# Attention, mixture of experts and a squared-ReLU network: eight squares put on another engine, and three groups of output weights prepared at earlier products

## The chip, the cores and the metric

The kernel runs on one core of one Trainium2 chip. The metric is the time of one execution on the device in microseconds (us). TensorE multiplies matrices, VectorE and GpSimd do element-wise work on tensors, ScalarE applies functions to them, and SyncE issues most of the transfers. Each engine takes its instructions strictly in the order of the program, and waits on semaphores for what other engines deliver.

## The reference: what is computed

Three networks follow one another: windowed attention (4 batches, 8 heads, 576 positions, width 64), a mixture of 8 experts with two chosen per token, and a dense network whose hidden values are squared after a ReLU. The change lies in the last one:

```python
def _moe2_ref(x, w_in, w_out):       # x 2304 x 512, w_in 512 x 2048, w_out 2048 x 512
    h = x @ w_in
    r = np.maximum(h, 0.0)
    g = r * r
    return (g @ w_out).astype(np.float32)
```

## The kernel before, in words

**Layers and products.** The last network works on three blocks of 768 tokens. Both of its layers use a recursive scheme with seven products in place of eight for a 2 x 2 split of the matrices. Its products are called 1 to 7 in the code, and their sums give four quarters of the result. Every operand is held as two numbers, a high part (a copy rounded on ScalarE) and a low part (the rest, mostly a subtraction on VectorE), so that each product is done in three passes: high by high, high by low, low by high. A high or low part is made by the operations that `split` (line 846) lists and `do` (line 870) issues, and so nearly all of these stand under line 872 in the profile.

**First layer.** The program walks 24 groups (3 blocks of 8, `NG`), seven products each. `product` (line 1155) does product "1" into PSUM tile `psa` and copies it to `tt` on ScalarE (line 1161), product "2" into `psc`, "6" on top of `psa` with a copy to `wt` (line 1169), "5" into `psb`, "7" on top of `psa` with a copy to `tt` (line 1176), "4" on top of `psa`, and "3" on top of `psb`. A product that adds to `psa` must wait until ScalarE has copied the sum before it. Each group gives four quarters, which are passed through ReLU and square and stored to DRAM (`gmid`). Three of them (quarters 0, 2 and 3, after products "2", "7" and "3") go through `g_sum` (line 1063): VectorE adds the PSUM tile and the copy (line 1065), and squares the positive part in place in one further VectorE instruction (line 1066). Quarter 1 (product "4") goes through two ScalarE instructions, Relu (line 1182) and Square (line 1183). A group's last two products, "4" and "3", stand among the first products of the next group; those of the last group come after all others.

**Second layer.** It takes 36 batches of 14 products (`mul_out`, line 1199), and reads as operands the stored quarters of two hidden groups (`g_load`, on SyncE's queue), their sums (`g_adds`, GpSimd), and the high and low parts of both (`g_split`: parts 0 and 2 on ScalarE, 1 and 3 on VectorE). Its buffers hold three batches. `g_split(n, 1)` also issues the load for batch n + 3.

**Slots.** What runs beside the products is set by hand. After each product `step` (line 1142) issues the side work listed under the number of that product, its slot. Product "1" of group g is slot 7g. The first layer's slots end at 167; the last products "4" and "3" follow without slots of their own; `end` = 168 is the first slot of the second layer, and batch n of it has slots 168 + 14n to 168 + 14n + 13. Side work of the same slot is issued in the order in which it was listed in the program.

**Output weights.** They are kept in eight groups, and take the places of the input weights of the same number. Each group is prepared in four pieces of 512, 512, 512 and 256 columns by eight steps (`w_sums`, line 892). An even step asks for the transfer of the piece after next (`w_load`, line 877, tile `raw`, on GpSimd's queue, four buffers) and makes the high part on ScalarE. An odd step makes the low part on VectorE. Groups 0 to 4 are done at slots 126 to 160 (line 1132), groups 5 to 7 at slots 168 + 20(k - 5) + (0, 2, 5, 7, 10, 12, 15, 17) for group k (lines 1211 and 1212). The low parts of group 5 so stand at slots 170, 175, 180 and 185, of group 6 at 190, 195, 200 and 205, of group 7 at 210, 215, 220 and 225. Batch 4 of the second layer needs group 5, batch 5 needs groups 6 and 7.

```python
    def g_sum(s, k, q, ps, u):
        t = g_tile()
        nc.vector.tensor_tensor(out=t, in0=ps, in1=u, op=OP.add)
        nc.vector.scalar_tensor_tensor(out=t, in0=t, scalar=0.0, in1=t, op0=OP.max, op1=OP.mult)
        g_to(s, k, q, t)
```

Of the kernel before, what the change touches and what calls it, by code (L numbers as in the profile page):

```python
# [16 lines left out]
AF = mybir.ActivationFunctionType  # L17
OP = mybir.AluOpType
# [31 lines left out]
def attn_moe_ffn(ctx: ExitStack, tc: tile.TileContext, qt, kt, vt, wgn, noise, w1, w2, w_in, w_out,  # L50
                 consts, out):
    nc = tc.nc
# [18 lines left out]
    def bank(tag):  # L71
        if tag == "b":
            return psum.tile([128, 2, 512], F32, name="psb", tag="b", bufs=2)
        return psum.tile([128, 512], F32, name="ps" + tag, tag=tag, bufs={"a": 3, "c": 1}[tag])
# [440 lines left out]
    for p in range(NT // 2):  # L515
        v = 4 * p + 3
        end = v == last
# [374 lines left out]
    def w_sums(k, out_w):  # L892

        steps = []
        for j in range(4):
            m, st = 4 * (8 * out_w + k) + j, {}

            def high(m=m, j=j, st=st):
                w_load(max(m + 3, 4))
                n_i = min(2, 7 - 2 * j)  # L900
                st[0] = split(WP[k], 2 * j, [w_buf(m)[:, 0:256 * n_i].rearrange("p (i n) -> p i n", n=256)], "dve")
                do(st[0][0])

            steps += [high, lambda st=st: do(st[0][1])]
        return steps
# [146 lines left out]
    NSB = N // SB  # L1052

    def g_to(s, k, q, t):
        nc.sync.dma_start(out=gmid[s, k, :, :, q, :].rearrange("u p n -> p u n"),
                          in_=t.rearrange("p (u n) -> p u n", u=3))

    def g_tile():
        ng[0] += 1
        n = (ng[0] - 1) % 4  # L1060
        return tmp[4 + n // 2] if n % 2 == 0 else rows.tile([128, DM], F32, name="yo", tag="yo", bufs=2)[:, 0:HALF]

    def g_sum(s, k, q, ps, u):
        t = g_tile()
        nc.vector.tensor_tensor(out=t, in0=ps, in1=u, op=OP.add)
        nc.vector.scalar_tensor_tensor(out=t, in0=t, scalar=0.0, in1=t, op0=OP.max, op1=OP.mult)
        g_to(s, k, q, t)


# [38 lines left out]
    def on(slot, f, *a):  # L1108
        side.setdefault(slot, []).append((f, a))

    def on_all(slots, steps):
        for m, f in zip(slots, steps):
            on(m, f)
# [3 lines left out]
    for s in range(NSB - 1):  # L1117
        for i in range(6):
            t, m = 6 * (s + 1) + i, 56 * s + 5 * i + 3
# [9 lines left out]
    out_sums = [w_sums(k, 1) for k in range(8)]  # L1129
    end = 56 * NSB  # L1130
    for k in range(5):
        on_all([end - 56 + 7 * (k + 2) + m for m in (0, 1, 2, 3, 3, 4, 5, 6)], out_sums[k])
    for n in range(3):
        on(end - 48 + 8 * n, g_load, n)
        for m in range(2):
            on(end - 20 + 4 * n + 2 * m, g_adds, n, "pool", m)
# [18 lines left out]
    def product(g, p):  # L1155
# [6 lines left out]
        elif p == "2":  # L1162
            b = bank("c")[:, :HALF]
            mul_in(P2, k, b, True, True)
            g_sum(s, k, 0, b, t)
        elif p == "6":
            a = LIVE["a", g]
            mul_in(P6, k, a, False, False)
            nc.scalar.activation(out=u2, in_=a, func=AF.Copy)
        elif p == "5":  # L1170
            LIVE["c", g] = c = bank("b")[:, 0, :HALF]
            mul_in(P5, k, c, True, False)
        elif p == "7":
            a = LIVE["a", g]
            mul_in(P7, k, a, False, False)
            nc.scalar.activation(out=u3, in_=a, func=AF.Copy)  # L1176
            g_sum(s, k, 2, LIVE["c", g], u3)
        elif p == "4":
            a = LIVE.pop(("a", g))
            mul_in(P4, k, a, False, True)  # L1180
            t = g_tile()
            nc.scalar.activation(out=t, in_=a, func=AF.Relu)
            nc.scalar.activation(out=t, in_=t, func=AF.Square)
            g_to(s, k, 1, t)
        else:
            c = LIVE.pop(("c", g))
            mul_in(P3, k, c, False, True)
            g_sum(s, k, 3, c, u2)
# [16 lines left out]
    for n in range(len(batches)):  # L1205
# [2 lines left out]
                on(end + 14 * n + 1 + 4 * m, g_adds, n + 3, "pool", m)  # L1208
        for m in range(4):
            on(end + 14 * n + (2, 5, 8, 11)[m], g_split, n + 2, m)  # L1210
    for k in range(5, 8):
        on_all([end + 20 * (k - 5) + m for m in (0, 2, 5, 7, 10, 12, 15, 17)], out_sums[k])
    BANKS = {}
    two = lambda ap: ap.rearrange("p (k n) -> p k n", k=2)
    twice = lambda ap: ap[:, None, :].to_broadcast([128, 2, 256])
    for n, (s, u, kk) in enumerate(batches):
        if kk == 0:
            if (3 * s + u) % 2:
                t = [bank("b") for _ in range(2)]
# [91 lines left out]
```

## Time and profile before

| What | Value |
|---|---|
| Time, median of 3 runs (lowest, highest) | 978.65 us (977.57, 979.04) |
| Profiled execution: time on the device | 978.19 us |
| Profiled execution: span from first to last instruction | 976.1 us |
| TensorE busy in the span | 957.3 us, 98% |
| VectorE busy | 674.8 us, 69% |
| ScalarE busy | 463.8 us, 48% |
| GpSimd busy | 419.2 us, 43% |
| Granted TensorE clock, mean over the span | 0.998 |

PE is TensorE, PEld its weight loads, DVE VectorE, ACT ScalarE, POOL GpSimd, SP SyncE. A row of the timeline gives the start in us from the span's start, the length in us, the engine, the line, the operation, output tile <- input tiles with their shapes, how many instructions are merged in the row, and in brackets how long the engine was idle before it and what ended that. An engine can begin an instruction a little before the one ahead has ended, so the distance between two starts is what an instruction costs its queue.

The first layer of the last network's third block (groups 16 to 23) runs from about 726 to 787 us; the second layer runs from 787 us to the end.

### The profile page before, as it was taken

The page shows a single profiled execution, that of the slowest core. Times are in us where ns is not written, and L with a number is a line of the kernel's source. Part 1 is how long each engine was busy: PE and PEld are TensorE (multiplying, and loading weights), DVE is VectorE, ACT ScalarE, POOL GpSimd, SP SyncE. Part 2 cuts the span into 40 slices and gives each one's busy share as a digit, 9 for nine tenths or more (in the row PEclk, how much of TensorE's full clock was granted, in tenths as well). Part 3 has the DMA queues.
Part 4 walks back from the last instruction along what each step waited for, and adds up shares of the span by engine and source line. Part 5 has one row for each costly group of instructions (what it writes and reads, how often), then busy time and mean ns, then how long its engine had stood idle before and what let it go on. Part 6 is the DMA issues. An engine that isn't in the chain of part 4 may idle for free. (4 is left out here: it accounts for less than half of the span.)

```text
span 976.1 us, 19647 instructions
## 1 busy us (share of the span) xinstructions
PE 957.3 (98%) x7438; PEld 879.1 (90%) x7438; DVE 674.8 (69%) x1432; ACT 463.8 (48%) x887; POOL 419.2 (43%) x453
## 2 busy tenths in 40 slices
PE   8899999999999999999999999999999999999998
PEld 6677779898998989899898898999999998999998
DVE  5777754757686776766764436778576999877773
ACT  6677743434343343433343446655554564434331
POOL 0665543124242333425334032624221667988880
PEclk9999999999999999999999999999999999999999
DMA  8777525456667575656555453976538774444331
GB/s 277 273 237 279 198 88 152 135 166 226 197 212 241 161 234 197 219 204 207 202 190 200 148 174 94 299 203 181 151 99 240 227 213 156 145 140 129 130 108 44
DMA packets 118198, 179.99 MB, mean 184 GB/s; under 512 B 11232, under 2 KB 66288, under 8 KB 117712
## 3 DMA queue, kind: packets, MB, share of 16 engines
q1 hardware_dynamic: 107120, 146.77, 46.9%
q0 software_dynamic: 10976, 31.90, 10.6%
q8 instruction: 59, 0.97, 0.4%
q14 instruction: 43, 0.35, 0.1%
HBM read 124.33 MB, written 54.30 MB: 183 GB/s over the span
## 5 line engine op out<-in xcount | busy, mean ns | idle before, releaser
L872 POOL TENSOR_TENSOR gs<-xb 128x256 f32<-128x256 f32 x72 | 69.5, 985 | 29.3 <-DVE wc L872 13.0
L476 ACT ACTIVATE ha<-psa 128x384 fp32r<-128x384 f32 x64 | 31.3, 491 | 93.3 <-PE psa L472 91.8
L268 ACT ACTIVATE p<-p,mx 128x192 f32<-128x192 f32 x144 | 57.6, 450 | 30.3 <-DVE mx L262 29.5
L689 POOL TENSOR_TENSOR et<-ex,et 128x512 f32<-128x512 f32 x16 | 20.9, 1304 | 112.3 <-DVE ex L685 112.3
L710 POOL DMA_INDIRECT yr<-yg,pos x36 | 36.1, 1003 | 68.4 <-DVE ha L477 44.9
L477 DVE SCALAR_TENSOR_TENSOR ha<-psa,ha 128x384 fp32r<-128x384 f32 x64 | 35.4, 553 | 43.0 <-ACT ha L476 38.0
L428 POOL DMA_INDIRECT slots<-tok,pos x36 | 35.0, 972 | 46.1 <-DVE rs L314 29.6
L472 PE MATMUL psa<-xa,wa 128*128 128x384 f32 x288 | 53.4, 336 | 0.3 <-DVE ha L477 0.3
L472 PE MATMUL psa<-xa,wc 128*128 128x384 f32 x288 | 53.4, 336 | 0.0
L791 PE MATMUL psb<-wa,ha 128*128 128x512 f32 x216 | 52.8, 396 | 0.0
L441 POOL DMA_INDIRECT xr<-xd,gidx x40 | 44.3, 1108 | 19.2 <-issue 6.0
L262 DVE CUSTOM_DVE_ANT_0 p<-psb,bias 128x192 f32<-128x192 f32 x144 | 45.8, 352 | 7.7 <-PE psb L257 6.8
L472 PEld LDWEIGHTS psa<-xa,wa 128*128 128x128 f32 x288 | 49.4, 188 | 0.6 <-DVE ha L477 0.5
L472 PEld LDWEIGHTS psa<-xa,wc 128*128 128x128 f32 x288 | 49.6, 188 | 0.2
L795 ACT ACTIVATE yo<-psb 128x512 f32<-128x512 f32 x38 | 22.7, 598 | 54.3 <-PE psb L791 40.8
L872 DVE TENSOR_TENSOR wc<-gs,wc 128x512 fp32r<-128x512 f32 x48 | 48.5, 1049 | 0.0
L689 POOL TENSOR_TENSOR ex<-ex 128x512 f32<-128x512 f32 x12 | 15.6, 1303 | 74.8 <-DVE ex L685 74.8
L886 POOL DMA_DIRECT2D raw<-w x49 | 27.2, 560 | 47.0 <-DVE wb L872 18.4
L791 PEld LDWEIGHTS psb<-wa,ha 128*128 128x128 f32 x216 | 39.5, 188 | 7.8
L791 PE MATMUL psb<-wb,ha 128*128 128x512 f32 x176 | 46.3, 398 | 0.0
L110 DVE TENSOR_TENSOR wa<-raw,wa 128x1024 fp32r<-128x1024 f32 x20 | 25.3, 1266 | 30.0 <-ACT wa L106 29.9
L303 PEld LDWEIGHTS psb<-v,pt 64*64 64x64 f32 (+1 forms) x1056 | 33.1, 136 | 11.6 <-issue 7.9
(327 smaller groups left out, 2742.6 us busy)
## 6 DMA issues: line engine op xcount, KB each, us to landing
raw<-in_w_dram SPq DMA_DIRECT2D x64, 512.0 KB, 5.3
xb<-gmid SPq DMA_DIRECT2D x72, 256.0 KB, 2.7
v<-in_vt_dram SPq DMA_DIRECT2D x20, 520.0 KB, 6.7
yg<-yo SPq DMA_DIRECT2D x40, 256.0 KB, 2.5
raw<-w POOLq DMA_DIRECT2D x36, 256.0 KB, 3.9
gmid<-yo SPq DMA_DIRECT2D x48, 192.0 KB
ex<-in_w_in_dram SPq DMA_DIRECT2D x16, 512.0 KB, 4.4
ex<-in_w_out_dram SPq DMA_DIRECT2D x16, 512.0 KB, 3.4
```

Of the source, the lines that this page charges most:

```text
L262: nc.vector.tensor_tensor_reduce(out=p2[j][:, a, :], in0=ps[:, a, j, :], in1=bias[:, 4 * g + 2 * j + a, :], op0=OP.add, op1=OP.min, scale= ...
L268: nc.scalar.activation(out=p2[j][:, a, :], in_=p2[j][:, a, :], func=AF.Exp, bias=mx[j][:, a:a + 1], scale=-1.0)
L303: nc.tensor.matmul(px[64 * x:64 * x + 64, a, j, :], l, r, start=not any(m[:2] == (x, a) for m in mms[:n]), stop=not any(m[:3] == (x, a, j) ...
L428: st = nc.gpsimd.indirect_dma_start(out=slots, out_offset=bass.IndirectOffsetOnAxis(ap=pos[:, i, k:k + 1], axis=0), in_=tok[:, i:i + 1], i ...
L441: nc.gpsimd.indirect_dma_start(out=XR[e, j], out_offset=None, in_=xd[0:PARTS[j] * 128] if early else xd, in_offset=bass.IndirectOffsetOnAx ...
L472: nc.tensor.matmul(o, w[wp][:, f * 128:(f + 1) * 128], x[:, xp, d, :], start=(n == 0), stop=(n == 11))
L476: nc.scalar.activation(out=hi, in_=ps, func=AF.Relu)
L477: nc.vector.scalar_tensor_tensor(out=lo, in0=ps, scalar=0.0, in1=hi.bitcast(F32), op0=OP.max, op1=OP.subtract)
L689: nc.gpsimd.tensor_tensor(out=x, in0=af, in1=cf, op=OP.add)
L710: nc.gpsimd.indirect_dma_start(out=YR[i, k], out_offset=None, in_=yg, in_offset=bass.IndirectOffsetOnAxis(ap=pos[:, i, k:k + 1], axis=0))
L791: nc.tensor.matmul(py, h[:, hq], wc[wp][:, wsl], start=(f + n == 0), stop=(f == 7 and n == 2))
L872: f(**a)
```

## The change

Two edits. In the third block, quarter 0 is no longer squared by one VectorE instruction but by a Relu and a Square on ScalarE, in place; VectorE keeps the addition ahead of them. And the steps of output-weight groups 5, 6 and 7 are listed under slots 161 + 21(k - 5) + (0, 2, 5, ...): group 5 seven slots sooner than before, group 6 six, group 7 five. They are also listed earlier in the program, so that in a slot shared with `g_load`, `g_adds` or `g_split` they now come first.

```diff
@@ -1063,7 +1063,11 @@
     def g_sum(s, k, q, ps, u):
         t = g_tile()
         nc.vector.tensor_tensor(out=t, in0=ps, in1=u, op=OP.add)
-        nc.vector.scalar_tensor_tensor(out=t, in0=t, scalar=0.0, in1=t, op0=OP.max, op1=OP.mult)
+        if s == NSB - 1 and q == 0:
+            nc.scalar.activation(out=t, in_=t, func=AF.Relu)
+            nc.scalar.activation(out=t, in_=t, func=AF.Square)
+        else:
+            nc.vector.scalar_tensor_tensor(out=t, in0=t, scalar=0.0, in1=t, op0=OP.max, op1=OP.mult)
         g_to(s, k, q, t)
 
 
@@ -1130,6 +1134,8 @@
     end = 56 * NSB
     for k in range(5):
         on_all([end - 56 + 7 * (k + 2) + m for m in (0, 1, 2, 3, 3, 4, 5, 6)], out_sums[k])
+    for k in range(5, 8):
+        on_all([end - 7 + 21 * (k - 5) + m for m in (0, 2, 5, 7, 10, 12, 15, 17)], out_sums[k])
     for n in range(3):
         on(end - 48 + 8 * n, g_load, n)
         for m in range(2):
@@ -1208,8 +1214,6 @@
                 on(end + 14 * n + 1 + 4 * m, g_adds, n + 3, "pool", m)
         for m in range(4):
             on(end + 14 * n + (2, 5, 8, 11)[m], g_split, n + 2, m)
-    for k in range(5, 8):
-        on_all([end + 20 * (k - 5) + m for m in (0, 2, 5, 7, 10, 12, 15, 17)], out_sums[k])
     BANKS = {}
```

## Rows read from the trace of the kernel before

**Rows 1.** Busy time by stage: PE, PEld, DVE, ACT, POOL, clock, DMA share, GB/s

```profile
773.00:787.10 14.10, 13.52 (x79) 13.20 (x78) 13.68 (x21) 9.10 (x19) 5.81 (x9) 1.00 0.79 229
787.10:807.00 19.90, 19.90 (x169) 19.90 (x168) 19.83 (x20) 12.09 (x22) 16.75 (x22) 1.00 0.65 192
807.00:820.10 13.10, 11.00 (x87) 10.36 (x86) 13.10 (x14) 7.01 (x14) 10.81 (x12) 1.00 0.34 111
```

**Rows 2.** All waits of TensorE from 780 us to the end: total us, times, longest

```profile
PE psa L1201 <- DVE ex L872: 1.2, 1, 1.2
PE psa L1201 <- DVE wc L872: 0.9, 1, 0.9
PE psa L1046 <- ACT tt L1176: 0.6, 1, 0.6
```

**Rows 3.** Timeline of TensorE, 775 to 821 us

```profile
775.66 1.20 PE L1046 MATMUL psa<-wc,wa 128*128 128x384 f32 x6
...
777.74 1.20 PE L1046 MATMUL psc<-wc,ha 128*128 128x384 f32 x6
...
784.73 1.34 PE L1046 MATMUL psa<-ex,ha 128*128 128x384 f32 x6 [0.58 <-ACT tt L1176]
...
786.94 1.59 PE L1201 MATMUL psa<-wb,wc 128*128 128x256 f32 x12
...
797.01 5.20 PE L1201 MATMUL psb<-wb,ex 128*128 128x256 f32 x42
...
820.13 2.68 PE L1201 MATMUL psb<-ha,wc 128*128 128x256 f32 x21
```

**Rows 4.** Timeline of ScalarE, 774 to 788 us

```profile
774.26 0.47 ACT L1169 ACTIVATE wt<-psa 128x384 f32<-128x384 f32 x1
...
780.07 0.49 ACT L1182 ACTIVATE yo<-psa 128x384 f32<-128x384 f32 x1 [1.64 <-PE psa L1046]
780.59 0.53 ACT L1183 ACTIVATE yo<-yo 128x384 f32<-128x384 f32 x1
781.02 0.83 ACT L872 ACTIVATE wc<-xb 128x768 fp32r<-128x768 f32 x1
781.76 0.47 ACT L1169 ACTIVATE wt<-psa 128x384 f32<-128x384 f32 x1
782.13 1.14 ACT L872 ACTIVATE wc<-gs 128x512 fp32r<-128x512 f32 x2
783.17 0.83 ACT L872 ACTIVATE wc<-xb 128x768 fp32r<-128x768 f32 x1
784.18 0.49 ACT L1176 ACTIVATE tt<-psa 128x384 f32<-128x384 f32 x1 [0.18 <-PE psa L1046]
...
787.05 0.62 ACT L872 ACTIVATE wa<-raw 128x512 fp32r<-128x512 f32 x1
```

**Rows 5.** Line 1066, 728 to 788 us: ns min/median/max, first and last start

```profile
L1066 DVE SCALAR_TENSOR_TENSOR tt<-tt x8: 557/558/1621, 729.4 to 781.2; 128x384 f32<-128x384 f32 x8
```

**Rows 6.** Timeline of VectorE, 772 to 817 us

```profile
772.93 0.55 DVE L1065 TENSOR_TENSOR tt<-psc,tt 128x384 f32<-128x384 f32 x1
...
773.99 2.12 DVE L872 TENSOR_TENSOR ha<-raw,ha 128x512 fp32r<-128x512 f32 x1
...
780.61 0.55 DVE L1065 TENSOR_TENSOR tt<-psc,tt 128x384 f32<-128x384 f32 x1
...
787.14 0.56 DVE L1065 TENSOR_TENSOR yo<-psb,wt 128x384 f32<-128x384 f32 x1
...
790.89 1.23 DVE L872 TENSOR_TENSOR wa<-raw,wa 128x512 fp32r<-128x512 f32 x1
...
816.18 0.95 DVE L872 TENSOR_TENSOR wa<-raw,wa 128x256 fp32r<-128x256 f32 x1
```

**Rows 7.** GpSimd's issue of a weight piece, and such transfers' time to landing

```profile
776.41 0.54 POOL L886 DMA_DIRECT2D raw<-w  x1 [0.86 <-DVE ha L872]
...
raw<-w POOLq DMA_DIRECT2D x6, 256.0 KB, 3.4
```

## The prediction

> **What bounds the kernel now.** I read the busy time by stage first [rows 1]. From 787.10 us, where the second layer begins, VectorE is busy for 19.83 of 19.90 us and then for all of 13.10 us, while ScalarE works 54 to 61% of the time; TensorE works through the first of these stretches without a gap and lacks 2.10 us in the second. So at the start of the second layer VectorE is the bound, and that is where the moved weight pieces stand. In the stretch ahead, 773 to 787 us, VectorE is nearly as full (13.68 of 14.10 us), yet TensorE loses only 0.58 us.
>
> The list of TensorE's waits says what these gaps are [rows 2]: two in the second layer, for low parts made by VectorE (0.9 us in batch 4, 1.2 us in batch 5), and one of 0.6 us at the end of the first, for ScalarE's copy of line 1176. No other wait of TensorE stands between 780 us and the end, so whatever shift remains when batch 6 begins is carried to the end. The timeline of TensorE bounds what can be won [rows 3]: from the start of batch 0 (786.94) to that of batch 6 (820.13) are 33.19 us. The first two, which lie ahead of both waits, take 10.07 us (batch 2 begins at 797.01), so six take 30.21 us with no wait. All that VectorE costs here is thus 2.98 us, and with the wait ahead of it 3.56 us, or 0.36%. What this kernel's measurement can tell from no change is about 0.2%, 1.96 us.
>
> One more reading carries the argument. VectorE's first instruction of the second layer's stretch is the sum for the last product "3" (787.14) [rows 6]. It starts 0.20 us after TensorE began on the second layer (786.94) [rows 3], as soon as that product has drained, though VectorE was all but full up to then. VectorE has caught up at this point, and what it saves earlier it would spend here, waiting for TensorE. I call this the meeting point, and count all that follows from it.
>
> **Squares moved.** Eight VectorE instructions of 0.558 us each in the median [rows 5] go, 4.5 us over a stretch of 52 us. Ahead of the meeting point that is worth nothing to TensorE, whose only loss there is to ScalarE [rows 1, 2]. What is added are eight pairs on ScalarE. The pair of lines 1182 and 1183 has the same tile: 0.52 us from the first start to the second, 0.43 us from there to the next instruction, 0.95 us together [rows 4]. Work of that size would fit into ScalarE's idle time. But the Relu has to wait for VectorE's sum, and everything listed behind it on ScalarE waits too. Among that are the copies for which TensorE's next product on `psa` waits (lines 1169 and 1176).
>
> In the last group, 23, this can be added up. Its product "2" begins at 777.74 and ends at 778.94 [rows 3]; VectorE adds only at 780.61 and is done at 781.16 [rows 6]. Until now ScalarE went on meanwhile: line 1182 at 780.07, line 1169 at 781.76, line 1176 at 784.18, done at 784.67 [rows 4]. With the change the queue from the sum's end to the end of line 1176 is, by distances of starts [rows 4]: Relu 0.52, Square 0.43, line 1182 0.52, line 1183 0.43, high part of batch 0's own operands 0.74, line 1169 0.37, its sums 1.04, the high part of group 5's second weight piece, now at slot 166, 0.53 (787.05 to the next row's start), batch 1's own high part 0.74, line 1176 itself 0.49: 5.81 us. From 781.16 that ends at 786.97, 2.30 us later than now. The last product "4" waits for just this copy (784.73, 0.58 us idle) [rows 3], and so the meeting point moves by 2.30 us.
>
> The end of the sum is the uncertain part. From below: VectorE has no backlog and adds as soon as product "2" ends, at 779.49; then the copy ends at 785.30, +0.63 us. With one square less ahead of it, 780.60: +1.74 us. From above: group 22 is itself held up. There the sum ends at 773.48 [rows 6]; Relu, Square, lines 1182 and 1183, a weight piece (0.53) and line 1169 (0.47) end at 776.38, where line 1169 now starts at 774.26, and the product that waits for it began at 775.66 [rows 3]: TensorE loses 0.7 us there, and the sum of group 23 can slip by as much, to 781.86: +3.0 us. I take 781.16: the 0.56 us saved are given back where VectorE's low part of a weight piece waits for its high part, which ScalarE brings 0.95 us later behind each added pair. The value 2.30 is nearest to the row as it stands.
>
> **Weight pieces moved.** Three things are moved: transfers, high parts, low parts. The transfer for the piece at slot 161 leaves GpSimd at 776.41 as before and lands 3.4 us later [rows 7], at 779.8; its high part (0.53) then ends at 780.3, ahead of the sum that ScalarE must wait for anyway, and costs nothing; if that transfer were 1.3 us later, it would cost up to 0.5 us. Its low part, at slot 163, falls where VectorE waits for ScalarE's late high part of batch 0. The later transfers are asked for sooner, and where GpSimd now waits for a low part before it goes on to sums for the next batches, those sums have slack: batch 3's stand at slots 169 and 173, its first product at 210. SyncE's queue gets no more transfers; the store of quarter 0 waits for the Square, and the load for batch 3 behind it waits for a low part that is itself 2 us late. I cost both at nothing, under VectorE's backlog.
>
> For the low parts I counted what stands in VectorE's queue between the meeting point and the part that holds batch 4 (slot 207) and batch 5 (slot 221). Before: up to 207 all of groups 5 and 6, eight pieces; up to 221 three more of group 7, eleven. After: group 5's first piece goes ahead of the meeting point (slot 163), but group 7 moves up too, to 205, 210, 215 and 220. Up to slot 207 three, four and one, again eight; up to 221 again eleven. The queue in front of the waits is no shorter, only a different piece: one of 1.23 us (790.89) goes, one of 0.95 us (816.18) comes [rows 6]. That is 0.28 us for batch 5. From the other side, if the piece that comes were hidden, the whole 1.23 us would be won.
>
> **Sum.** 2.30 - 0.28 = 2.02 us on the profiled execution, whose own time is 978.19 us: 980.2 us. That execution lies 0.46 us under the median of the runs, 978.65; set against the median the sum gives **980.7 us**. From the ends: 0.63 - 1.23 = -0.6 us, or 978.1; 3.0 us and no gain behind it, 981.7.
>
> Of the pages, the Trainium skill, "ScalarE: Activation LUTs", section "Rules for kernel authors", speaks against the first edit: relu and multiplications belong on VectorE. The rows agree as to size, 0.95 us on one engine for 0.56 us on the other; they do not show its reason, a faster mode of VectorE. Were all eight exchanges on the path, the loss by it would be 8 x 0.39 = 3.1 us; by the rows only the last group's place in the queue counts.
>
> **Rivals.** *ScalarE has room and VectorE is relieved (not slower).* For it: ScalarE is busy 9.10 of 14.10 us where VectorE is full [rows 1]. It decides at group 23's sum: if that ends by 779.5 us, because eight squares less leave VectorE no backlog, the meeting point moves by 0.63 us only and 0.28 to 1.23 us come back behind it: 978.1 to 979.0 us, no change. Against it: VectorE's backlog at that point, 1.1 us at the least (781.16 against 779.49, less one square), comes from low parts that take up to 2.12 us beside GpSimd's sums (773.99) [rows 6], and not from squares. The Trainium skill, "Perfetto Trace Analysis", section "Optimizing Scalar/DVE Operations", would have it this way: offload to ScalarE where VectorE is saturated. Here that would hold only as far as the offloaded half does not wait on the saturated one.
>
> *The waits of batches 4 and 5 go (faster).* The low parts after the meeting point run at 1.23 us where an undisturbed square of three quarters of their width takes 0.558 us; if GpSimd's sums come ahead of them, VectorE's queue shrinks by enough for all 2.98 us. Less 0.63 us this gives 976.3 us. Against it: GpSimd's sums wait for loads that hang on the same late low parts, so they move along with the meeting point.
>
> *ScalarE and VectorE hold each other in more groups (slower still).* VectorE waits for high parts, ScalarE for sums. If the groups ahead, 17 to 22, each cost TensorE 0.3 us that nothing later absorbs, 1.8 us come on top: 982.5 us.
>
> *The second edit does nothing.* By the count of pieces that is nearly my forecast; the first alone would then give 2.30 us, 981.0 us.
>
> **How the numbers follow.** The forecast with its bounds, the second edit's idleness included, has 0.62; the relieved VectorE 0.20; the faster case 0.10; the mutual hold 0.08. The range of 8 in 10, 977.4 to 982.2 us, takes in the forecast from 978.1 to 981.7, the relieved case and part of the two outer ones. Slower by over 0.2% means above 980.6 us, and the predicted value lies just on its far side: of the forecast's 0.62 I put 0.40 above and 0.22 within, with the mutual hold above: slower 0.48. Faster means under 976.7 us: the faster case and a little of the relieved one, 0.11. Within: 0.41.
>
> **What would show it.** In the changed kernel's profile ScalarE should wait for VectorE's line 1065 ahead of the new Relu, 1 to 2 us in groups 22 and 23; TensorE's wait for line 1176 should grow from 0.58 to about 2.9 us, less what line 1169 already took as a new wait; the second layer should begin near 789.2 us; from there to batch 6 should be near 32.9 us, with the waits for `wc` and `ex` still there. The forecast is wrong if the second layer begins before 787.8 us, if that stretch falls under 32 us, or if TensorE waits in groups 16 to 21.

## The result, and the profile after

The changed kernel took 983.69 us in the median of 7 runs (979.87 to 986.01) against 978.65 us before (977.45 to 979.75, 7 runs): 1.0054 times as long, with a 95% interval from 1.0038 to 1.0070. It is slower by some 5 us. The direction was forecast; the size, 2.0 us, was not, and the median lies above the range given (977.4 to 982.2).

The engines' busy time in the profiled execution of the changed kernel, from its page:

```profile
PE 957.5 (98%) x7438; PEld 877.7 (90%) x7438; DVE 668.1 (68%) x1424; ACT 470.2 (48%) x903; POOL 419.0 (43%) x453
```

VectorE did 6.7 us less than before and ScalarE 6.4 us more. The profiled execution took 979.87 us, the fastest of the seven, and seems to have lost little. That is misleading, as the timeline of TensorE shows when it is laid beside that of before. First the kernel before, product "2" of group 16, which is still untouched by either edit:

```profile
726.78 1.20 PE L1046 MATMUL psc<-wc,wb 128*128 128x384 f32 x6
```

Then the changed kernel: the same product, product "2" of groups 21, 22 and 23 with what stopped TensorE around them, the start of the second layer, and batch 6 of it:

```profile
723.37 1.20 PE L1046 MATMUL psc<-wc,wb 128*128 128x384 f32 x6
...
759.83 1.20 PE L1046 MATMUL psc<-wc,wa 128*128 128x384 f32 x6
...
765.87 2.38 PE L1046 MATMUL psa<-wc,wa 128*128 128x384 f32 x12 [0.68 <-ACT wt L1175]
768.09 1.20 PE L1046 MATMUL psc<-wc,wa 128*128 128x384 f32 x6
...
776.15 1.31 PE L1046 MATMUL psa<-wc,wa 128*128 128x384 f32 x6 [2.70 <-ACT wt L1175]
...
778.34 1.20 PE L1046 MATMUL psc<-wc,ha 128*128 128x384 f32 x6
...
786.41 1.32 PE L1046 MATMUL psa<-ex,ha 128*128 128x384 f32 x6 [1.34 <-ACT tt L1182]
...
788.61 1.59 PE L1207 MATMUL psa<-wb,wc 128*128 128x256 f32 x12
...
822.14 2.68 PE L1207 MATMUL psb<-ha,wc 128*128 128x256 f32 x21
```

This execution happened to reach group 16 3.41 us sooner than the profiled execution of before (723.37 against 726.78), in work that the change doesn't touch. From there on both can be compared, and I use two stretches for all that follows. The **first stretch** runs from product "2" of group 16 to the start of the second layer: 726.78 to 786.94 = 60.16 us before, 723.37 to 788.61 = 65.24 us after. The **second stretch** runs from there to batch 6: 33.19 us before [rows 3], 33.53 us after. Together 93.35 and 98.77 us: the change costs 5.42 us where it acts, 5.08 of them in the first stretch. What follows batch 6 takes 155.97 us before and 155.96 after.

The list of TensorE's waits from 700 us to the end, for the changed kernel (total us, times, longest); before, [rows 2] were all there was in its last 196 us:

```profile
PE psa L1046 <- ACT wt L1175: 3.4, 2, 2.7
PE psa L1207 <- DVE wc L872: 1.4, 1, 1.4
PE psa L1046 <- ACT tt L1182: 1.3, 1, 1.3
PE psb L1207 <- DVE wc L872: 0.3, 1, 0.3
```

Two waits for line 1175 (1169 before), 0.68 us in group 21 and 2.70 us in group 22, are new, and the one for line 1182 (1176 before) has grown from 0.58 to 1.34 us. All three are for ScalarE's copies. What ScalarE itself waited for, and VectorE, stands in their own lists, ScalarE's from 720 us and VectorE's from 735 us, both to just behind the start of the second layer, changed kernel:

```profile
ACT tt L1067 <- DVE tt L1065: 11.4, 8, 3.9
...
DVE wb L872 <- ACT wb L872: 4.0, 2, 2.0
...
DVE hb L872 <- ACT hb L872: 2.0, 1, 2.0
DVE xa L872 <- ACT xa L872: 2.0, 1, 2.0
DVE ha L872 <- ACT ha L872: 2.0, 1, 2.0
...
DVE yo L1065 <- PE psb L1046: 0.2, 1, 0.2
```

and VectorE's list for the same groups before:

```profile
DVE wb L872 <- ACT wb L872: 1.8, 2, 0.9
DVE hb L872 <- ACT hb L872: 0.9, 1, 0.9
...
DVE xa L872 <- ACT xa L872: 0.2, 1, 0.2
```

ScalarE waits 11.4 us for VectorE's eight sums, and in five groups VectorE in turn waits 2.0 us for one high part of the output weights from ScalarE, where it waited 0.9 us or less before. The change frees VectorE of 0.56 us per group and makes it stand still for 1 to 2 us more.

### The profile page after: what moved, and what is told of

Same layout as the page of the kernel before. It is cut to its first block, busy times and chain, and to the rows that moved or that the text cites. A ratio compares the mean times of both kernels' runs of the same rounds, so it can differ in the third digit from the quotient of the medians.

```text
span 978.1 us, 19636 instructions
## 1 busy us (share of the span) xinstructions
PE 957.5 (98%) x7438; PEld 877.7 (90%) x7438; DVE 668.1 (68%) x1424; ACT 470.2 (48%) x903; POOL 419.0 (43%) x453
## 5 line engine op out<-in xcount | busy, mean ns | idle before, releaser
L872 POOL TENSOR_TENSOR gs<-xb 128x256 f32<-128x256 f32 x72 | 67.4, 957 | 31.3 <-DMA xb<-gmid 13.4
```

The lines of the kernel that those rows point to most:

```text
L872: f(**a)
```

## Experiments

Two theories stood against each other. Theory 1: the Relu waits in ScalarE's queue for VectorE's late sum, and the copies and high parts behind it wait too. Theory 2: the weight pieces brought forward crowd the stretch ahead of the second layer (or ScalarE's added work as such does).

The experiments ran on four chips, and each ratio is to the kernel before on the same chip. On the first two the kernel before took 1009.07 us (35 runs) and 1005.62 us (35 runs), with a scatter of 13 us from run to run; on the last two 977.94 us (23 runs) and 977.92 us (17 runs). The extra time lies ahead of the last network's third block (in the run of the weight pieces alone, product "2" of group 16 starts at 755.40 us), so beside each ratio I give the two stretches of the profiled execution, worked out from starts as above. Rows of those timelines are shown only where a verdict hangs on them. Each pair of stretches is one trace. Two traces of the same kernel, three times in the table, differ by 1.04, 1.45 and 0.30 us in the first stretch and by 0.40, 1.15 and 0.50 us in the second; smaller differences than these decide nothing.

| Kernel | Ratio to before (95% interval) | First stretch, us | Second, us | Both |
|---|---|---|---|---|
| before | | 60.16 | 33.19 | 93.35 |
| the change | 1.0054 (1.0038 to 1.0070) | 65.24 | 33.53 | 98.77 |
| the change again | 1.0033 (1.0008 to 1.0057) | 66.28 | 33.13 | 99.41 |
| squares alone | 1.0031 (1.0004 to 1.0058) | 65.10 | 34.35 | 99.45 |
| squares alone, again | 1.0061 (1.0045 to 1.0076) | 66.55 | 33.20 | 99.75 |
| weight pieces alone | 0.9989 (0.9959 to 1.0019) | 60.40 | 34.10 | 94.50 |
| pair later, five slots in the last group | 1.0027 (1.0001 to 1.0053) | 60.86 | 36.62 | 97.48 |
| pair two slots later | 1.0008 (0.9981 to 1.0036) | 62.86 | 32.86 | 95.72 |
| change, GpSimd's sums early | 1.0022 (0.9993 to 1.0051) | 65.35 | 33.21 | 98.56 |
| group 5 alone sooner | 0.9996 (0.9970 to 1.0022) | 60.41 | 32.94 | 93.35 |
| group 5 ahead, sums early | 0.9978 (0.9950 to 1.0007) | 61.68 | 31.49 | 93.17 |
| groups 0 to 5 five slots sooner, sums early | 0.9996 (0.9979 to 1.0014) | 62.42 | 30.62 | 93.04 |
| the same, sums kept | 0.9981 (0.9966 to 0.9997) | 62.65 | 31.12 | 93.77 |
| the same, again | 0.9987 (0.9974 to 1.0001) | 62.35 | 30.62 | 92.97 |

**Squares alone.** The first hunk of the change without the other two.

> First edit alone. Theory 1 (the Relu's place in ScalarE's queue: it waits for VectorE's late sum, and the copies that TensorE needs wait behind it): nearly the whole loss is here, 3.5 to 5.5 us above before, with TensorE waiting for lines 1175 and 1182 for 3 us or more. Theory 2 (the weight pieces brought forward crowd ScalarE, VectorE and the transfers ahead of the meeting point): at most 1 us above before.

The first stretch took 65.10 us, with TensorE's waits for ScalarE nearly those of the changed kernel:

```profile
PE psa L1046 <- ACT wt L1173: 3.5, 2, 2.7
...
PE psa L1046 <- ACT tt L1180: 0.8, 1, 0.8
...
```

The runs of that chip scatter too widely for a size, so the same kernel ran once more on a quieter one:

> The first edit alone once more, in the same call, since its runs came from a chip with a scatter of 8 us. By its first trace it costs 6 us over before from group 16 to batch 6 (99.45 against 93.35), with nearly all of it ahead of the second layer. If this is right, the runs are 4 to 7 us above before and the first stretch is 65 to 66.5 us again, with a weight piece's high part listed behind the pair reaching VectorE 2 us late in each of groups 18 to 21.

983.51 us against 977.92, 5.6 us more, and 66.55 us in the first stretch, with VectorE's waits of 2.0 to 2.4 us for a high part as expected. The first edit alone costs as much as both, so the crowding by weight pieces falls.

**Weight pieces alone.** The second and third hunk without the first.

> Second edit alone. Theory 1: within 0.6 us of before, since the count of low parts ahead of the waits of batches 4 and 5 is the same, eight and eleven. Theory 2: 3 to 5 us above before.

0.9989, no difference that can be told. The first stretch is as before but for 0.24 us. In the second, batch 5's wait is gone, batch 4's is 1.4 us instead of 0.9, and batch 3 has one of 0.9 us:

```profile
PE psa L1203 <- DVE wc L872: 1.4, 1, 1.4
PE psb L1203 <- DVE wc L872: 0.9, 1, 0.9
...
```

So the second edit shifts which batches wait and wins nothing that can be told; the 0.91 us by which the second stretch is longer here are within what two traces of one kernel differ by. Batch 3's wait is not the edit's alone: it stands with 0.8 us also in the first trace of the squares alone.

**The same pair, later.** The work stays on ScalarE; only its place in the queue changes.

```diff
         if s == NSB - 1 and q == 0:
-            nc.scalar.activation(out=t, in_=t, func=AF.Relu)
-            nc.scalar.activation(out=t, in_=t, func=AF.Square)
+            on(slot[0] + (5 if k == 7 else 2), g_square, s, k, q, t)
         else:
...
+    def g_square(s, k, q, t):
+        nc.scalar.activation(out=t, in_=t, func=AF.Relu)
+        nc.scalar.activation(out=t, in_=t, func=AF.Square)
+        g_to(s, k, q, t)
```

> Both edits, but ScalarE's Relu and Square are listed two slots later (behind line 1169's copy; in the last group five slots later, behind line 1176's copy as well). The same work on the same engines, only its place is changed. Theory 1: the loss goes, from 1.2 us under before to 0.6 us over it, and TensorE's waits on ScalarE's copies stay under 1 us. Theory 2, or ScalarE's added work as such: 3 to 5 us above before, as with the change.

The expected total was missed, and the expected mechanism hit: the first stretch is 60.86 us, 4.4 us shorter than with the change, with one wait of 0.9 us in it. But the second stretch lost 3.4 us to a wait that I had put there myself. ScalarE's timeline at the end of the first layer:

```profile
810.95 0.52 ACT L1073 ACTIVATE tt<-tt 128x384 f32<-128x384 f32 x1
...
818.53 0.49 ACT L1192 ACTIVATE tt<-psa 128x384 f32<-128x384 f32 x1 [6.51 <-DMA gmid<-tt]
```

The last group's quarter 1 (product "4", line 1192 here) takes the buffer of the pair four tiles earlier, and as the pair came five slots late, ScalarE waited 6.51 us for that buffer's store, and TensorE 4.2 us for ScalarE. With two slots in the last group as well:

> Both edits, the Relu and Square two slots later in every group, the last one too (so the buffer of quarter 0 is stored in time, which it was not in the run with five slots in the last group). Measured from product 2 of group 16 to the second layer's start (60.16 us before, 65.24 with the change) and from there to batch 6 (33.19 and 33.53). Theory 1 (place in the queue): 60.9 to 61.8 us for the first, under 34.3 for the second, so 1 to 2.5 us over before in all. Theory 2 (ScalarE's added work as such): 63 us or more for the first.

62.86 and 32.86 us, 2.4 us over before instead of 5.4. Between the two expectations for the first stretch (under 61.8, or 63 and more), nearer to the second; the timeline says why. All groups up to 23 keep their pace, and the loss begins with one wait of 2.04 us at the very end, for line 1186 (1176 before): in the last group the pair (0.97 us by starts) and one high part (0.52 us), which the second edit brought there, still stand in front of that copy. Behind this wait TensorE's granted clock fell to 0.50, from about 812 to 816 us and so across the end of the stretch (see the last section); part of the 2.70 us is the clock and not the queue.

```profile
808.73 0.51 ACT L1073 ACTIVATE tt<-tt 128x384 f32<-128x384 f32 x1
...
809.70 0.61 ACT L872 ACTIVATE wa<-raw 128x512 fp32r<-128x512 f32 x1
810.22 0.83 ACT L872 ACTIVATE wc<-xb 128x768 fp32r<-128x768 f32 x1
810.95 0.47 ACT L1186 ACTIVATE tt<-psa 128x384 f32<-128x384 f32 x1
```

Theory 1 holds: the same instructions on the same engines cost 5 us of the first stretch in one place of the queue, and 0.7 and 2.7 us in others. This rests on one trace of each: by the ratios the kernel with two slots (1.0008) can't be told from the change on the same chip (1.0033), and the one with five lost its gain elsewhere. The squares alone were not tried in a later place.

**GpSimd's sums moved away.** Does the loss need them?

```diff
-        on(end - 48 + 8 * n, g_load, n)
+        on(end - 48 + 3 * n, g_load, n)
         for m in range(2):
-            on(end - 20 + 4 * n + 2 * m, g_adds, n, "pool", m)
+            on(end - 42 + 4 * n + 2 * m, g_adds, n, "pool", m)
```

> Both edits, and GpSimd's sums for batches 0 to 2 moved from slots 148 to 158 to slots 126 to 136 (their loads from 120, 128, 136 to 120, 123, 126). If the hold between ScalarE and VectorE becomes a loss only where GpSimd's sums slow VectorE as well, the first stretch falls from 65.2 to 61 to 63 us, and VectorE's squares near the end last 0.56 us and not 2 us. If the Relu's place is enough by itself, it stays at 64 to 66 us.

65.35 us: the loss stays. But it moves. With the change TensorE lost time from group 21 on; here it lost most of it between product "2" of groups 19 and 20, which start 11.41 us apart instead of 7.28, and only 0.3 us in the three groups after:

```profile
778.63 1.20 PE L1046 MATMUL psc<-wc,xa 128*128 128x384 f32 x6
...
786.56 1.76 PE L1046 MATMUL psa<-wc,hb 128*128 128x384 f32 x6 [2.56 <-ACT wt L1175]
...
790.04 1.49 PE L1046 MATMUL psc<-wc,ha 128*128 128x384 f32 x6
```

So the loss does not hang on where GpSimd's sums stand, but it moves along with them, three groups ahead. Its size is not quite the same: behind the gap of 2.56 us the granted clock fell to 0.50 here, from about 787 to 791 us, and did not in the first profile of the change. Against the change again, where it fell too (66.28 us), this stretch is 0.9 us shorter, no more than two traces of one kernel differ by. The sums were moved within the stretch and not taken out of it, so whether the Relu's place alone would be enough, or only together with them, is not shown.

**Group 5 alone sooner.** Of the second edit only `out_sums[5]` moved, no squares.

> Of the second edit only group 5 is brought forward by seven slots, groups 6 and 7 stay; no squares moved. The low parts between the meeting point and slots 207 and 221 are then seven and ten, one fewer than before. If the queue behind the meeting point sets the waits of batches 4 and 5, it gains 0.6 to 1.2 us; if the piece ahead of the meeting point delays the copies there, or the waits hang on something else (transfers, GpSimd's sums), it is within 0.4 us of before.

Within 0.4 us of before: the second stretch is 0.25 us shorter, the first as much longer, and neither can be told from nothing. One low part fewer in VectorE's queue did not give the 1.23 us of its row [rows 6]. I read this as follows: that row holds time in which GpSimd's sums slowed it, and when the piece is taken away the sums slow what comes in its place. This was not tried by itself.

**More of the weights ahead of the second layer.** From the kernel before, no squares moved: all of group 5 at slots 161 to 167 and GpSimd's sums early (as in the diff above).

> The kernel before with GpSimd's sums for batches 0 to 2 at slots 126 to 136 and all four pieces of weight group 5 ahead of the meeting point (slots 161 to 167), groups 6 and 7 as before; no squares moved. First stretch 60.2 to 61.5 us (ScalarE has four more high parts ahead of line 1176's copy), second stretch 31.0 to 32.5 us (four low parts fewer in VectorE's queue, 0.3 to 0.6 us each). In all between 1.5 us under before and 0.3 us over.

Second stretch 31.49 us, four pieces fewer for 1.70 us, 0.43 us each; but the first lost 1.52 us. Of these 1.03 us fall behind the last product "2", where TensorE's wait for line 1176, with the added high parts in front of it, grew from 0.58 to 1.6 us. To get these out of the way, all groups were begun five slots sooner, with the sums early and with the sums kept in their place:

```diff
-    for k in range(5):
-        on_all([end - 56 + 7 * (k + 2) + m for m in (0, 1, 2, 3, 3, 4, 5, 6)], out_sums[k])
+    for k in range(6):
+        on_all([end - 61 + 7 * (k + 2) + m for m in (0, 1, 2, 3, 3, 4, 5, 6)], out_sums[k])
...
-    for k in range(5, 8):
+    for k in range(6, 8):
```

> The kernel before with output-weight groups 0 to 5 five slots sooner (group 5 at slots 156 to 162) and GpSimd's sums for batches 0 to 2 at slots 126 to 136; groups 6 and 7 and all squares as before. If the loss of the run with group 5 ahead of the meeting point (first stretch 61.7 us) was its high parts in front of line 1176's copy, the first stretch comes back to 60.2 to 60.8 us and the second stays at 31.3 to 31.8: 1.0 to 1.8 us under before. If VectorE's own load there was the cause, the first stretch stays over 61.3 us.

> The same, with GpSimd's sums for batches 0 to 2 left at slots 148 to 158. If room on VectorE ahead of the meeting point has to be made by moving these sums, the first stretch rises to 61.5 us or more, or TensorE waits for line 1169 or 1176 by 1.5 us; if not, it is as in the run before this one, within 0.4 us.

> The last kernel once more. Its runs gave 0.9981 of before (0.9966 to 0.9997), its one trace 0.4 us more than before from group 16 to batch 6. If the gain is real the ratio again comes out under 0.9995 and the trace shows where; if it is the scatter of the time before group 16, the ratio is within 0.15% of 1.

The sums' place makes no difference to the totals that can be told. The second stretch falls to 30.62 us, all but free of waits (six batches take 30.21). The first did not come back to 60.8 as expected, but stayed at 62.4, which by the expectation would mean VectorE's own load. ScalarE's timelines show something else in front: a weight piece of group 5 that waits for its transfer, with line 1176's copy right behind it. First the kernel with the sums kept:

```profile
778.78 0.63 ACT L872 ACTIVATE wa<-raw 128x512 fp32r<-128x512 f32 x1 [3.17 <-DMA raw<-w]
779.31 0.47 ACT L1176 ACTIVATE tt<-psa 128x384 f32<-128x384 f32 x1
```

and the same kernel again, with GpSimd's issue of that transfer:

```profile
774.51 0.54 POOL L886 DMA_DIRECT2D raw<-w  x1 [1.07 <-issue]
...
777.74 0.63 ACT L872 ACTIVATE wa<-raw 128x512 fp32r<-128x512 f32 x1 [3.06 <-PE psc L1046]
```

The second row names a product of TensorE (product "2" of group 23, slot 162), but that stands behind this piece (slot 159) in the program, so the piece cannot wait for it. The piece starts 3.23 us after GpSimd issued the transfer, and in the first trace that transfer took 3.2 us. With the sums early, ScalarE's waits for such transfers, 2.78, 3.07 and 2.07 us, stand ahead of three of these copies between product "2" of groups 19 and 22, and the first stretch loses its time there and not at the end. So the high parts came up ahead of their transfers. What held these (GpSimd's queue, or buffers that VectorE frees late) was not tried by itself.

The kernel with the sums kept measured 0.9981 (0.9966 to 0.9997) and 0.9987 (0.9974 to 1.0001) of before: 1.4 to 1.8 us faster than before, and by the ratios some 5 to 7 us faster than the change. The two intervals all but exclude no gain, but 0.9987 fits both answers that were expected of it; the stretches of its traces (93.77 and 92.97 against 93.35) don't show where so much would come from, and this stays open.

**The change again,** for the scatter of its runs.

> The changed kernel once more, for its trace and the runs' scatter. If the gap between its profiled execution (979.87 us) and the median of its runs (983.69) comes from the time before the last network's third block, the two stretches come out as in the first profile, 65.2 and 33.5 us, within 0.7 us. If it comes from the stretches of the change, they differ by 2 us or more.

66.28 and 33.13 us: 1.04 us from the first profile in the first stretch, between the two answers, and the last section says what the 1.04 us are. The first profile's gap to the median fits the head start of 3.41 us: 979.87 + 3.41 = 983.28 us, and the median is 983.69. But the other six runs also had a mean granted clock of 0.996 to 0.997 against 0.999 in the profiled one, so part of the gap can be falls of the clock that the first profile happened to lack; how it divides is not shown.

## Why the prediction was right in sign and wrong in size

**What held.** VectorE and TensorE do meet at the start of the second layer (VectorE waits 0.2 us for TensorE there, the last row of its list), and squares taken off VectorE ahead of it gained nothing that can be told (second stretch 33.53 and 33.13 us against 33.19). The Relu's place in ScalarE's queue is the cause, shown by the squares alone and by the pair placed later. The queue of the last group was added up to 5.81 us from the sum's end to the end of the copy before the last product "4"; ScalarE's timeline of the changed kernel has the Relu at 780.56, right behind that sum, and the copy from 785.88, ending at 786.36:

```profile
780.56 0.53 ACT L1067 ACTIVATE tt<-tt 128x384 f32<-128x384 f32 x1 [1.01 <-DVE tt L1065]
...
785.88 0.48 ACT L1182 ACTIVATE tt<-psa 128x384 f32<-128x384 f32 x1
```

That is 5.80 us. The second edit's count of pieces, eight and eleven, is not contradicted: no gain by it alone that can be told.

**What failed** is one step, the end of VectorE's sum, for which the Relu waits: "the 0.56 us saved are given back where VectorE's low part of a weight piece waits for its high part". They are given back several times over. The forecast put the whole loss, 2.30 us, into group 23 and nothing into the groups ahead. By distances of starts the stretch lost 0.98 us in group 21 (768.09 - 759.83 against 7.28), 2.97 in group 22 (10.25 against 7.28) and 1.07 in group 23 (10.27 to the second layer against 9.20). I had let the wait for the high part cancel the saved square and left group 22's sum where it was, 1.82 us after its product "2" had ended (771.66 to 773.48). The rows of groups 21 and 22 show what happens. VectorE first:

```profile
762.32 0.55 DVE L1065 TENSOR_TENSOR tt<-psc,tt 128x384 f32<-128x384 f32 x1
762.79 0.68 DVE L872 TENSOR_TENSOR xa<-raw,xa 128x512 fp32r<-128x512 f32 x1
765.47 0.96 DVE L872 TENSOR_TENSOR xa<-raw,xa 128x512 fp32r<-128x512 f32 x1 [2.00 <-ACT xa L872]
...
766.94 2.22 DVE L1070 SCALAR_TENSOR_TENSOR et<-et 128x384 f32<-128x384 f32 x1
...
772.61 0.55 DVE L1065 TENSOR_TENSOR tt<-psc,tt 128x384 f32<-128x384 f32 x1
```

and ScalarE in the same time:

```profile
762.90 0.53 ACT L1067 ACTIVATE tt<-tt 128x384 f32<-128x384 f32 x1 [1.86 <-DVE tt L1065]
763.46 0.53 ACT L1068 ACTIVATE tt<-tt 128x384 f32<-128x384 f32 x1
763.89 0.47 ACT L1188 ACTIVATE yo<-psa 128x384 f32<-128x384 f32 x1
...
764.83 0.61 ACT L872 ACTIVATE xa<-raw 128x512 fp32r<-128x512 f32 x1
765.35 0.47 ACT L1175 ACTIVATE wt<-psa 128x384 f32<-128x384 f32 x1
...
768.67 0.62 ACT L872 ACTIVATE ha<-raw 128x512 fp32r<-128x512 f32 x1
773.18 0.52 ACT L1067 ACTIVATE tt<-tt 128x384 f32<-128x384 f32 x1 [3.89 <-DVE tt L1065]
```

and GpSimd's sums:

```profile
767.29 1.44 POOL L872 TENSOR_TENSOR gs<-xb 128x256 f32<-128x256 f32 x2
```

ScalarE waits 1.86 us for group 21's sum, then does the pair, then quarter 1, and only then the high part; VectorE has meanwhile done its one ready piece and stands idle for 2.00 us. Held up like this it runs into GpSimd's sums (767.29 to 768.73), where a square takes 2.22 us and not 0.56. So group 22's sum ends at 773.16, 3.87 us after its product (768.09 + 1.20), ScalarE stands idle for 3.89 us, and TensorE for 2.70 us. My upper bound had 0.7 there, with the sum 1.82 us after the product; with the 2.05 us by which it came later, 0.7 + 2.05 = 2.75. So ScalarE's queue was right there too, and the time of the sum was wrong. Group 21 adds a wait of 0.68 us, where I had nothing; a wait in groups 16 to 21 was among the signs that I had named for being wrong. In group 23 the sum comes promptly, 0.98 us after its product and not 2.22, since TensorE had lost so much; so that group lost less than forecast. By the list of waits the sum is 0.68 + 2.70 + 1.34 - 0.58 = 4.14 us; the stretch lost 5.08. I read the rest as the first matmuls behind each gap, whose rows are longer than the usual 1.20 us, and gaps too short for the list.

In the groups 18 to 20 VectorE stood idle for 2.0 us each as well, but TensorE lost nothing: there the queue had room. Up to that point every margin that I had looked at was kept, which is why I gave the rival in which the two engines hold each other only 0.08. It was the one that came true, in groups 21 and 22, though not in the form in which I priced it (0.3 us in each of six groups). The sign that I should have followed stood in my own text: each added pair brings the next high part 0.95 us later. I used that to cancel a gain, and did not carry it on to the next group's sum.

**The second stretch** was forecast to win 0.28 us and lost 0.34, or won 0.06 the second time; neither can be told from nothing. The price of a low part, 1.23 us by its row, was too high: four fewer gave 0.43 us each.

**The level of the runs** holds one trap: a profiled execution that reached group 16 by chance 3.4 us sooner. Against the profiled execution of before the change would have looked like 1.7 us (979.87 against 978.19). The forecast for this execution, 980.2 us, and the sign that the second layer should begin near 789.2 us (788.61) look like hits for the same reason. They are luck: without the head start of 3.41 us the second layer would begin at 792.02.

## What to carry to other kernels

Before an operation is moved to an engine with idle time, look at what it waits for and at what stands behind it in that engine's queue: half an operation that waits for the engine it is to relieve stops everything behind it, and if the first engine needs some of that, both stand still. Share of busy time does not show this; the order of the two queues does. And a duration read from an engine that is slowed by another is not what taking that operation away is worth.

## What the runs showed of the hardware

**The clock after a gap.** In five of the seven traces with a TensorE gap of 2 us or more in these stretches the granted clock fell to 0.50, the lower of its two levels (1.2 GHz), behind it; in the other two, the first profile of the change and the first of the squares alone, it did not, behind a gap of the same 2.7 us. None of the traces without such a gap shows it. The change again, stretches of 2 us around its gap of 2.69 us (columns as in [rows 1]):

```profile
798.00:800.00 2.00, 0.68 (x4) 0.35 (x3) 0.97 (x2) 1.53 (x4) 1.55 (x3) 1.00 0.47 133
800.00:802.00 2.00, 0.63 (x2) 0.63 (x3) 1.03 (x1) 2.00 (x5) 1.91 (x4) 0.75 0.73 202
802.00:804.00 2.00, 2.00 (x8) 2.00 (x7) 1.84 (x4) 0.45 (x2) 1.29 (x2) 0.50 0.55 157
```

Product "2" of groups 22 and 23 start 11.65 us apart there (793.31 and 804.96) and 10.25 us in the first profile (768.09 and 778.34), for a gap of the same length: the clock cost 1.4 us. This is the 1.04 us between the two profiles of the change, and more. In the two traces of the squares alone the same distance is 11.22 us with the fall and 10.25 without, 0.97 us. So a gap of 2.7 us can cost 4. The Trainium skill, "TensorE: Matmul & The Clock Gate", section "Part 1: The HAM clock gate", says that the clock is set by how busy the engine has been of late; the rows agree, and show besides that the same gap does not always bring it about.

**VectorE beside GpSimd.** Squares of one shape, SBUF to SBUF, take 0.56 us in the median and up to 2.22 us beside GpSimd's sums. The Trainium skill, "Perfetto Trace Analysis", section "Optimizing Scalar/DVE Operations", says that the two share a read port of SBUF; the rows agree. The sums on line 1065, which read one operand from PSUM, stay between 0.54 and 0.56 us in the whole first stretch, before and after, also beside GpSimd's sums.
